# Attention backward on one core: halves of X's transposes in iterations 2 and 6, part G behind the transposes in three iterations, Z one step later, loads at other steps

## The chip, the core and the metric

The kernel runs on one core of a Trainium2 chip. The core has a matrix engine (PE, whose weight loads are shown as PEld), a vector engine (DVE), a scalar engine (ACT), a general engine (POOL) and a sequencer that issues DMAs (SP). Each engine works through its own instructions in the order in which the program lists them; between engines, order comes from semaphores only. The metric is the device time of one execution in microseconds, as a median of several runs.

## The reference

A gated attention block and its gradient, in bf16. `x` is 2048 x 512, there are 32 heads of 16 columns, and a feed-forward branch of 1792 gates the attention. The kernel returns the output and the gradients with respect to seven inputs.

```
def _A_ref(x, wqkv, wo):
    qkv = (x @ wqkv) split into 3, heads of 16
    scores = einsum("bhqd,bhkd->bhqk", q, k) * (Dh ** -0.5)
    p = softmax(scores)
    o = einsum("bhqk,bhkd->bhqd", p, v)
    return o @ wo
def _fwd_reference(...):
    xn = layernorm(x)
    s = _A_ref(xn, A_wqkv, A_wo)
    g = silu(layernorm-MLP of xn)
    return x + s * g
_out, _vjp = jax.vjp(_f, A_x, A_wqkv, A_wo, B_w1, B_b1, B_w2, B_b2)
_grads = _vjp(grad_out)
```

What matters here is the middle of the kernel: for each head, the 2048 x 2048 matrix of exponentials E, the matrix G = E * (dO V^T), and the sums over both that give the attention's output and the gradients of q, k and v.

## The kernel before

Three stages follow one another: a stage that makes q, k, v and the gate (up to 219 us), the attention (`attention_core`, from 219 to about 1867 us), and the weight gradients (`Grads.run`). The change is in the attention alone.

The attention works on pairs of heads (16 pairs) and, for each pair, on four groups of 512 queries: 64 **blocks**. A block has 16 **iterations**, one for each 128 keys (`kb`). The loop at L1382 runs over `g`, the number of the iteration over all blocks; "iteration k" below means `g % 16 == k`. The loop writes the order of all engines' work out by hand. In iteration g it emits, in this order:

- `emit_cO(g - 2)` (L1226): two DVE copies (L1233) of 128x64 words, for some g only ("older", below).
- `emit_xt(g - 1)` and `emit_fin(g - 1)`: for two g of a block, a DVE copy of a transposed half of X (L1292) and POOL's work on it (L1313 to L1331), which makes the weights W1 and W2 of Z.
- `emit_d` and `emit_s`: four PE products d, s, s, d with 32-row weights (L1137, L1115). s is of the next unit, g + 1; d is dO V^T of unit g. s has one PSUM tile; d has three in turn.
- `emit_exp(g + 1)`: ACT's exponential (L1124) into `ets`, which holds E of the last twelve units.
- `emit_z(g + ZOFF)` (L1352): four PE products Z with 32-column weights W on the transposed G (`gk`) and E (`ek`, `ekd`) of a unit 20 iterations back. Eight steps sum into one PSUM tile.
- `emit_x(g - 1, part)`: twelve PE products into X, in three parts: "e" (E with k and v, L1250, here called E part), "l" (row sums, L1253, L part) and "g" (the product tile `gts` of unit g - 1, L1257, G part). In iteration 1 all three come after the transposes instead of before them.
- `emit_T(g - 1)` (L1208): seven of the eight 128x128 transposes of unit g - 1's E, into the PSUM tile `tT`, of which there is one. `emit_XT(g)` (L1284) puts two fp32 transposes of a half of X into the second half of the same tile.
- `emit_mult(g)`: two DVE products (L1153), `gts` = d * E. Between the two, in some iterations, DVE copies X out (`emit_xs`, L1266, iteration 0) or adds Z to its accumulator (`emit_acc`, L1364 and L1366, when eight Z steps are done).
- Loads that are due: POOL reads a corner of `gts` (`tick`, L1422), so that it waits for unit g, and issues one DMA for the operands of the next pair of heads.
- `emit_cT(g - 1)` (L1224): ACT's copy of the transposes from `tT` to `ek`; and `emit_dmat(g)`: DMA transposes that SP issues, of G (`gk`, L1170, every second iteration) and of the tiles of E that PE leaves out (`ekd`, L1180 to L1186, at units 4, 6, 12 and 14).

Since `tT` has one buffer, the transposes of an iteration can start only when everything that reads the tile of the iteration before is done: ACT's copy, DVE's older copies and the copy of the half of X.

Two functions make room for the halves of X. `cut(g)` says for which units the first three transposes are left out, so that half of `tT` is free; `OLDER` says in which later units those three tiles are made up, one each, as an eighth transpose (L1211), and DVE copies that one and its neighbour (`emit_cO`). Units 16 and up do this, so the first block has neither.

```
OLDER = {2: (0, 0), 4: (0, 1), 5: (0, 2), 6: (3, 0), 7: (3, 1), 8: (3, 2)}
def cut(g):
    return 3 if g >= 16 and g % 16 in (0, 3) else 0
FIN_AT = {1: 1, 4: 0}
ZOFF = -20
```

The keys of `OLDER` are units; a unit u is transposed in iteration u + 1 and its older tile is copied by DVE in iteration u + 2. So eight transposes stand in iterations 3, 5, 6, 7, 8 and 9, four and a half of X in 1 and 4, and DVE's older copies in 4 and 6 to 10. `ZOFF` sets when Z of a block begins (iteration 4 of the next block) and so when a sum of eight is complete: in iterations 3 and 11.

The loads for the next pair are spread over its four blocks, four to a block, due at iterations 6, 9, 12 and 15 (L1395): 13 for most pairs, 128 KB each for the two `NATQ` tiles, 64 KB for most others, 264 KB for `NAT`. In the first block of a pair POOL also stores the finished gradients (L1370, L1373) behind the two accumulations.

Of the kernel before, what the change touches and what calls it, by code (L numbers as in the profile page):

```python
# [69 lines left out]
def natq_loads(k, t, p, ld):  # L70
    return [lambda n=n, d=d: ld(out=t[n][:].rearrange("q k j c -> q k (j c)"), in_=d[p])
            for n, d in (("NATQq", k.NATQq_s), ("NATQd", k.NATQd_s))]
# [978 lines left out]
def attention_core(ctx, ctx_r, tc, k, grads, Oall, dQall, dKVT_out, ident_f32, ident_bf, npairs=16, nqc=4):  # L1051
    nc = tc.nc
# [36 lines left out]
    st_s, st_d, st_et, st_gt, st_T = {}, {}, {}, {}, {}  # L1089
# [3 lines left out]
    def a_unit(g):  # L1093
        return (g // 16, g % 16) if 0 <= g < NSTEP else None
# [6 lines left out]
    def op_of(j):  # L1101
        return OP[blocks[j][0] % 2]
# [16 lines left out]
    def emit_exp(g):  # L1119

        a = a_unit(g)
        if a is None:
            return
        nc.scalar.activation(out=st_et[g][:, :, :, a[1] % 4, :].rearrange("k b h q -> k h b q"),  # L1124
                             in_=cur["s"][:].rearrange("k h (b q) -> k h b q", b=4), func=ACT.Exp)

    def emit_d(g, hj):
        a = a_unit(g)
        if a is None:
            return  # L1130
        j, kb = a
        op = op_of(j)
        qc = blocks[j][1]
        r = 64 + 32 * hj
        d = ps_d.tile([128, 512], f32, name="d", tag="d")
        st_d[g, hj] = d
        nc.tensor.matmul(d[:], lhsT=op["KVT"][r:r + 32, kb * 128:(kb + 1) * 128], rhs=op["QDT"][r:r + 32, qc * 512:(qc + 1) * 512],  # L1137
                         start=True, stop=True, tile_position=(r, 0))


    def emit_mult(g):
        a = a_unit(g)
        if a is None:
            emit_xs(g - 1)
            emit_acc(g + ZOFF)
            return
# [5 lines left out]
        for hj in range(2):  # L1152
# [3 lines left out]
            if hj == 0:  # L1156
                emit_xs(g - 1)
                emit_acc(g + ZOFF)

# [27 lines left out]
                                            in_=ets[:].rearrange("k s b h a q -> k (s b h) (a q)")[:, 8 * sl - 1:8 * sl + 1]  # L1187
                                            .rearrange("k x q -> k (x q)"))

    OLDER = {2: (0, 0), 4: (0, 1), 5: (0, 2), 6: (3, 0), 7: (3, 1), 8: (3, 2)}  # L1190

    def cut(g):
        return 3 if g >= 16 and g % 16 in (0, 3) else 0

    def older(g):
        return OLDER.get(g % 16) if 16 <= g < NSTEP else None

    def emit_T(g):
        a = a_unit(g)
        if a is None:  # L1200
            return
        kk = a[1] % 4
        et = st_et[g]
        t = ps_t.tile([128, 512], f32, name="tT")
        tb = t[:].bitcast(bf16).rearrange("q (i k) -> q i k", k=128)
        for i in range(cut(g), 7):
            b = i + a[1] // 4 % 2
            nc.tensor.transpose(tb[:, i - cut(g), :], et[:, b // 2, b % 2, kk, :], ident_bf[:])  # L1208
        if older(g):
            kk2, b = older(g)  # L1210
            nc.tensor.transpose(tb[:, 7, :], st_et[g // 16 * 16 + kk2][:, b // 2, b % 2, kk2, :], ident_bf[:])  # L1211
        st_T[g] = t
        if kk == 0:
            cur["ek"] = ekc.tile([128, 4, 7, 128], bf16, name="ek")
            blk[a[0]]["Ek"][a[1] // 4] = cur["ek"]
# [11 lines left out]
    def emit_cO(g):  # L1227
        if a_unit(g) is None or not older(g):
            return
        j, kb = a_unit(g)  # L1230
        kk, i = older(g)
        for (kc, x, y), c in (((kb // 4, kb % 4, 6), 384), ((0, kk, i), 448)):
            nc.vector.tensor_copy(out=blk[j]["Ek"][kc][:, x, y].bitcast(f32), in_=st_T[g][:, c:c + 64])  # L1233

    def emit_x(g, part):
        a = a_unit(g)
        if a is None:
            return
        j, kb = a
        if part == "e" and kb == 0:  # L1240
            blk[j]["X"] = ps_x.tile([128, 512], f32, name="X", tag="X")
        X = blk[j]["X"]
        NATt = op_of(j)["NAT"]
        et = st_et[g]
        for c in range(4):
            half, hj = c // 2, c % 2
            r = 32 * c
            ev = et[:, half::2, hj, kb % 4, :]
            if part == "e":
                nc.tensor.matmul(X[r:r + 32, 0:256], lhsT=NATt[:, kb, hj, 1:33], rhs=ev,  # L1250
                                 start=(kb == 0), stop=False, skip_group_check=True, tile_position=(0, r))
            elif part == "l":
                nc.tensor.matmul(X[r:r + 32, 256:512], lhsT=Lc[:], rhs=ev,  # L1253
                                 start=False, stop=False, skip_group_check=True, tile_position=(0, r))
            else:
                gv = st_gt[g][:, kb % 2, hj, :].rearrange("k (b q) -> k b q", b=4)[:, half::2, :]
                nc.tensor.matmul(X[r:r + 17, 256:512], lhsT=NATt[:, kb, hj, 0:17], rhs=gv,  # L1257
                                 start=False, stop=(kb == 15), skip_group_check=True, tile_position=(0, r))

    def emit_xs(g):  # L1260
        a = a_unit(g)
        if a is None or a[1] != 15:
            return
        j = a[0]
        xs = xsp.tile([128, 512], f32, name="xs", tag="xs")
        nc.vector.tensor_copy(out=xs[:], in_=blk[j].pop("X")[:])  # L1266
        blk[j]["xs"] = xs

    def fin_half(g):
        j = g // 16 - 1  # L1270
        at = FIN_AT if j < NB - 1 else FIN_END
        return (j, at[g % 16]) if 0 <= j < NB and g % 16 in at else None
# [14 lines left out]
    def emit_xt(g):  # L1287
        f = fin_half(g)
        if f is None:
            return  # L1290
        j, h = f
        nc.vector.tensor_copy(out=blk[j]["xs"][:, 256 * h:256 * h + 256], in_=blk[j].pop("XT"))  # L1292
# [62 lines left out]
    def emit_acc(g):  # L1355
        u = z_unit(g)
        if u is None or u[2] != 3 or u[3] != 1:
            return
        j, kp = u[0], u[1]
        p, qc = blocks[j]  # L1360
        Z = blk[j]["Z"]
        av = acc[:, kp, :]
        if qc == 0:
            nc.vector.tensor_copy(out=av, in_=Z[:])  # L1364
        else:
            nc.vector.tensor_tensor(out=av, in0=Z[:], in1=av, op=ALU.add)  # L1366
        if qc == nqc - 1:
            ob = (outp.tile([128, 512], bf16, name="ob") if kp == 0 or j < NB - 1 else
                  xsp.tile([128, 512], bf16, name="ob", tag="xs"))
            nc.gpsimd.tensor_copy(out=ob[:], in_=av)  # L1370
            dv = dKVT_out[p * 64:(p + 1) * 64, :].rearrange("r (a b s) -> r a b s", a=2, b=2)
            for b in range(2):
                nc.gpsimd.dma_start(out=dv[:, kp, b, :], in_=ob[b * 64:(b + 1) * 64, :])  # L1373

    FIN_AT = {1: 1, 4: 0}
    FIN_END = {1: 1, 2: 0}
    ZOFF = -20
    late = []
    for hj in range(2):
        emit_s(0, hj)  # L1380
    emit_exp(0)
    for g in range(NSTEP - ZOFF):  # L1382
        cur["g"] = g
        a = a_unit(g)
        if a is not None:
            j, kb = a
            p, qc = blocks[j]
            if kb == 0 and qc == 0:
                L = natq_loads(k, k.op0, p, nc.gpsimd.dma_start) if p > 0 else []
                if p + 1 < npairs:  # L1390
                    L += op_load_list(k, OP[(p + 1) % 2], p + 1, nc.gpsimd.dma_start)
                else:
                    L += grads.tail_loads(nc.gpsimd.dma_start)
                for i, f in enumerate(L):
                    late.append((g + 16 * (i // 4) + 6 + 3 * (i % 4), f))  # L1395
        emit_cO(g - 2)
        if a_unit(g - 2) is not None:
            emit_xt(g - 1)
            emit_fin(g - 1)
        emit_d(g, 0)  # L1400
        emit_s(g + 1, 0)
        emit_s(g + 1, 1)
        emit_d(g, 1)
        emit_exp(g + 1)
        emit_z(g + ZOFF)
        if g % 16 != 1:
            for part in "elg":
                emit_x(g - 1, part)
        st_T.pop(g - 2, None)
        emit_T(g - 1)  # L1410
        emit_XT(g)
        if g % 16 == 1:
            for part in "elg":
                emit_x(g - 1, part)
        emit_mult(g)
        if a_unit(g - 1) is None:
            emit_xt(g)
            emit_fin(g)
        for it in [x for x in late if x[0] <= g]:
            late.remove(it)  # L1420

            nc.gpsimd.tensor_copy(out=tick[:], in_=st_gt[g][0:1, kb % 2, 1, 510:512])  # L1422
            it[1]()
        if g >= NSTEP:
            grads.tail_mid(g - NSTEP)
        emit_cT(g - 1)
        emit_dmat(g)
        st_gt.pop(g - 2, None)
        st_et.pop(g - 12, None)
        if g == NSTEP:  # L1430
            ctx_r.close()
            grads.tail_open(ps_t, ps_s, ps_d)
# [113 lines left out]
```

## Time and profile before

| what | value |
|---|---|
| median of 3 runs | 2196.99 us (2195.66 to 2199.49) |
| profiled execution | 2192.31 us, span 2190.3 us |
| granted PE clock over the span | 0.998 |
| attention, first d of block 0 to first d of block 63 | 218.6 to about 1829.2 us |
| mean block, blocks 2 to 61 | 25.55 us, of it DVE 24.2, ACT 23.1, POOL 6.4 busy |
| DMA moved | 461.14 MB, most of it by SP's transposes |

The block and iteration times are read from the starts of the d products (L1137) in the trace: an iteration runs from its first d to the next iteration's first d. A busy PE is not a PE at its peak, since matmuls overlap and their ends are modelled; so starts are compared, not lengths. Idle time of an engine that nobody waits for costs nothing.

### The profile page before, as it was taken

The numbers are of one execution on the slowest core, as the hardware profiler recorded it, in microseconds if no ns is written. First come the engines' busy times: TensorE is split into PE (matmuls) and PEld (weight loads), VectorE is DVE, ScalarE is ACT, GpSimd is POOL, SyncE is SP. The second block draws the span as 40 slices with busy tenths as digits, with TensorE's granted clock in tenths as the row PEclk, the third lists the DMA queues.
The fourth block names the chain that finished last, engine by engine and source line by source line (L and its number), as shares of the span: only waits on it lengthen the run. The fifth ranks groups of instructions, "written<-read, shape, count | busy, mean of one in ns | idle before, by whom it ended". The sixth has DMA issues, their size and how long they took to land.

```text
span 2190.3 us, 74125 instructions
## 1 busy us (share of the span) xinstructions
PE 2138.8 (98%) x30610; PEld 1159.2 (53%) x30659; DVE 1937.1 (88%) x3901; ACT 1769.5 (81%) x2481; POOL 597.0 (27%) x1373
## 2 busy tenths in 40 slices
PE   6999999999999999999999999999999999899999
PEld 3444555555555555555555555555555555444444
DVE  6677899999999999999999999999999999798647
ACT  5664889998989999989999899999899998685224
POOL 4376213221222222222223222222222222611003
PEclk9999999999999999999999999999999999999999
DMA  7786999999999999999999999999999999999975
GB/s 234 247 279 202 199 201 196 200 200 200 196 202 201 201 203 202 201 191 209 193 202 206 194 202 205 196 206 202 200 197 206 192 215 201 311 260 231 248 214 179
DMA packets 1422035, 461.14 MB, mean 211 GB/s; under 512 B 1334591, under 2 KB 1405887, under 8 KB 1421697
## 3 DMA queue, kind: packets, MB, share of 16 engines
q1 hardware_dynamic: 1407392, 425.46, 103.0%
q0 software_dynamic: 12720, 29.37, 4.8%
q8 instruction: 240, 3.93, 0.8%
q10 hardware_dynamic: 1584, 1.57, 0.2%
q14 instruction: 99, 0.80, 0.1%
HBM read 62.79 MB, written 64.75 MB: 58 GB/s over the span
## 4 chain that ended last, share of the span: by engine, by line
PE 90%; DMA 4%; DVE 2%; ACT 2%; issue 1%; SPq 0%; POOL 0%; ACTq 0%; DVEq 0%; POOLq 0%
PE tT L1208 22%; PE Z L1352 15%; PE d L1137 15%; PE X L1257 5%; PE X L1250 5%; PE X L1253 5%; PE s L1115 3%; PE ps_dy L909 2%; DMA ekd<-ets 2%; PE ps_dw L983 2%; PE ps_h L352 2%; PE ps_m L367 2%; PE ps_dw L742 2%; PE ps_dh L875 2%; PE tT L1284 1%; PE ps_dxa L1027 1%
## 5 line engine op out<-in xcount | busy, mean ns | idle before, releaser
L1153 DVE TENSOR_TENSOR gts<-d,ets 128x512 bf16<-128x512 f32 x2048 | 1305.2, 681 | 73.0 <-issue 23.4
L1124 ACT ACTIVATE ets<-s 128x1024 bf16<-128x1024 f32 x1024 | 1049.3, 1025 | 44.7 <-ACT ek L1224 26.7
L1224 ACT COPY ek<-tT 128x448 f32<-128x448 f32 (+2 forms) x1024 | 504.8, 493 | 113.7 <-PE tT L1208 14.7
L1208 PE MATMUL tT<-ident_bf,ets 128*128 128x128 bf16 x6790 | 557.6, 221 | 0.0
L1208 PEld LDWEIGHTS <-ets 128*128 128x128 bf16 x6790 | 382.7, 98 | 223.3 <-issue 129.7
L1137 PE MATMUL d<-QDT,KVT 32*128 32x512 bf16 x2048 | 462.5, 383 | 0.0
L1115 PE MATMUL s<-QDT,KVT 32*128 32x512 bf16 x2048 | 401.4, 381 | 9.0 <-ACT ets L1124 9.0
L1257 PE MATMUL X<-gts,NAT 128*17 128x256 bf16 x4096 | 299.9, 273 | 0.0
L1250 PE MATMUL X<-ets,NAT 128*32 128x256 bf16 x4096 | 290.8, 274 | 0.0
L1253 PE MATMUL X<-ets,Lc 128*32 128x256 bf16 x4096 | 289.9, 273 | 0.0
L1352 PEld LDWEIGHTS <-W 128*32 128x32 bf16 x4096 | 105.4, 93 | 235.8 <-issue 233.6
L1352 PE MATMUL Z<-gk,W 128*32 128x512 bf16 x2048 | 203.6, 389 | 1.2 <-DVE acc L1366 1.0
L1352 PE MATMUL Z<-ek,W 128*32 128x512 bf16 x1792 | 203.6, 389 | 0.0
L1137 PEld LDWEIGHTS <-KVT 32*128 32x128 bf16 x2048 | 140.2, 91 | 117.7 <-issue 24.9
L1422 POOL COPY tick<-gts 1x2 bf16<-1x2 bf16 x205 | 36.2, 176 | 539.3 <-DVE gts L1153 535.0
L1253 PEld LDWEIGHTS <-Lc 128*32 128x32 bf16 x4096 | 109.8, 97 | 102.5
L1115 PEld LDWEIGHTS <-KVT 32*128 32x128 bf16 x2048 | 134.0, 91 | 22.8 <-issue 17.1
L1233 DVE COPY ek<-tT 128x64 f32<-128x64 f32 x756 | 133.9, 219 | 12.0 <-ACT ek L1224 1.4
L1313 POOL TENSOR_TENSOR W<-NATQq,rL 128x128 bf16<-128x128 bf16 x64 | 25.4, 398 | 428.9 <-DVE rL L1312 364.9
L1257 PEld LDWEIGHTS <-NAT 128*17 128x17 bf16 x4096 | 112.9, 91 | 13.7 <-issue 0.3
L1250 PEld LDWEIGHTS <-NAT 128*32 128x32 bf16 x4096 | 108.1, 96 | 15.0 <-issue 15.0
L1352 PE MATMUL Z<-ekd,W 128*32 128x512 bf16 x256 | 99.7, 389 | 0.0
(252 smaller groups left out, 2462.6 us busy)
## 6 DMA issues: line engine op xcount, KB each, us to landing
gk<-gts SPq DMA_TRANSPOSE x512, 5.4
H1T_s<-h1r SPq DMA_DIRECT2D x28, 256.0 KB, 4.3
HGT_s<-hgT SPq DMA_DIRECT2D x8, 896.0 KB, 4.4
DH_s<-stg SPq DMA_DIRECT2D x12, 512.0 KB, 3.7
hch<-DH_s SPq DMA_DIRECT2D x12, 512.0 KB, 5.3
gp<-H1T_s SPq DMA_DIRECT2D x9, 512.0 KB, 7.7
out_dram<-ob_w POOLq DMA_DIRECT2D x36, 128.0 KB, 4.4
NAT_s<-NS SPq DMA_DIRECT2D x4, 1056.0 KB, 6.2
```

What stands on the lines that cost most here:

```text
L352: nc.tensor.matmul(ps[:], lhsT=w1_sb[:, ic, fc * 128:(fc + 1) * 128], rhs=yT[:, ic, g * 512:(g + 1) * 512], start=(ic == 0), stop=(ic == I ...
L1115: nc.tensor.matmul(s[:, hj, :], lhsT=op["KVT"][r:r + 32, kb * 128:(kb + 1) * 128], rhs=op["QDT"][r:r + 32, qc * 512:(qc + 1) * 512], start ...
L1124: nc.scalar.activation(out=st_et[g][:, :, :, a[1] % 4, :].rearrange("k b h q -> k h b q"), in_=cur["s"][:].rearrange("k h (b q) -> k h b q ...
L1137: nc.tensor.matmul(d[:], lhsT=op["KVT"][r:r + 32, kb * 128:(kb + 1) * 128], rhs=op["QDT"][r:r + 32, qc * 512:(qc + 1) * 512], start=True, ...
L1153: nc.vector.tensor_tensor(out=gts[:, kb % 2, hj, :].rearrange("k (b q) -> k b q", b=4), in0=st_d.pop((g, hj))[:].rearrange("k (b q) -> k b ...
L1208: nc.tensor.transpose(tb[:, i - cut(g), :], et[:, b // 2, b % 2, kk, :], ident_bf[:])
L1224: nc.scalar.copy(out=blk[j]["Ek"][kb // 4][:, kb % 4, c:hi].rearrange("q i k -> q (i k)").bitcast(f32), in_=st_T[g][:, 0:(hi - c) * 64])
L1233: nc.vector.tensor_copy(out=blk[j]["Ek"][kc][:, x, y].bitcast(f32), in_=st_T[g][:, c:c + 64])
L1250: nc.tensor.matmul(X[r:r + 32, 0:256], lhsT=NATt[:, kb, hj, 1:33], rhs=ev, start=(kb == 0), stop=False, skip_group_check=True, tile_positi ...
L1253: nc.tensor.matmul(X[r:r + 32, 256:512], lhsT=Lc[:], rhs=ev, start=False, stop=False, skip_group_check=True, tile_position=(0, r))
L1257: nc.tensor.matmul(X[r:r + 17, 256:512], lhsT=NATt[:, kb, hj, 0:17], rhs=gv, start=False, stop=(kb == 15), skip_group_check=True, tile_pos ...
L1352: nc.tensor.matmul(Z[r:r + 32, :], lhsT=WT[j % 2][1 - part][:, qb, hj, :], rhs=mv, start=(part == 0 and qb == 0), stop=(part == 1 and qb = ...
```

## The change

Five things change, all in `attention_core`:

- The transposed halves of X go from iterations 1 and 4 to iterations 2 and 6 (`FIN_AT`), so the units that leave out three transposes are 1 and 5 instead of 0 and 3 (`cut`).
- Their three tiles each are made up in units 3, 6, 7 (of unit 1) and 8, 9, 11 (of unit 5) instead of 2, 4, 5 and 6, 7, 8. The indices in `emit_T` and `emit_cO` are generalized, because unit 5 is not in the first group of four.
- X: parts E and L always come before the transposes. Part G comes before them too, except in iterations 1, 5 and 13, where it comes after. Before, iteration 1 had all three after.
- `ZOFF` is -21, so each Z step comes one iteration later, the accumulations come in iterations 4 and 12, and the loop has one more step at its end.
- The loads of a block are due at iterations 4, 5, 11 and 12.

```
-    OLDER = {2: (0, 0), 4: (0, 1), 5: (0, 2), 6: (3, 0), 7: (3, 1), 8: (3, 2)}
+    OLDER = {3: (1, 0), 6: (1, 1), 7: (1, 2), 8: (5, 0), 9: (5, 1), 11: (5, 2)}

     def cut(g):
-        return 3 if g >= 16 and g % 16 in (0, 3) else 0
+        return 3 if g >= 16 and g % 16 in (1, 5) else 0
...
         if older(g):
-            kk2, b = older(g)
-            nc.tensor.transpose(tb[:, 7, :], st_et[g // 16 * 16 + kk2][:, b // 2, b % 2, kk2, :], ident_bf[:])
+            kk2, i = older(g)
+            b = i + kk2 // 4 % 2
+            nc.tensor.transpose(tb[:, 7, :], st_et[g // 16 * 16 + kk2][:, b // 2, b % 2, kk2 % 4, :], ident_bf[:])
...
-        for (kc, x, y), c in (((kb // 4, kb % 4, 6), 384), ((0, kk, i), 448)):
+        for (kc, x, y), c in (((kb // 4, kb % 4, 6), 384), ((kk // 4, kk % 4, i), 448)):
...
-    FIN_AT = {1: 1, 4: 0}
+    FIN_AT = {2: 1, 6: 0}
     FIN_END = {1: 1, 2: 0}
-    ZOFF = -20
+    ZOFF = -21
...
-                    late.append((g + 16 * (i // 4) + 6 + 3 * (i % 4), f))
+                    late.append((g + 16 * (i // 4) + (4, 5, 11, 12)[i % 4], f))
...
         emit_z(g + ZOFF)
-        if g % 16 != 1:
-            for part in "elg":
-                emit_x(g - 1, part)
+        emit_x(g - 1, "e")
+        emit_x(g - 1, "l")
+        if g % 16 not in (1, 5, 13):
+            emit_x(g - 1, "g")
         st_T.pop(g - 2, None)
         emit_T(g - 1)
         emit_XT(g)
-        if g % 16 == 1:
-            for part in "elg":
-                emit_x(g - 1, part)
+        if g % 16 in (1, 5, 13):
+            emit_x(g - 1, "g")
```

## The prediction

> **What bounds the kernel now.** I read the page first, then the waits, then one block of 16 iterations engine by engine, and last the DMA that ACT sometimes waits for. The first fence is from the page: engine totals, and the chain that ended last.
>
> ```profile
> span 2190.3 us, 74125 instructions
> PE 2138.8 (98%) x30610; PEld 1159.2 (53%) x30659; DVE 1937.1 (88%) x3901; ACT 1769.5 (81%) x2481; POOL 597.0 (27%) x1373
> ...
> PE 90%; DMA 4%; DVE 2%; ACT 2%; issue 1%; SPq 0%; POOL 0%; ACTq 0%; DVEq 0%; POOLq 0%
> ```
>
> PE carries the chain, so what counts is the order of PE's work and what holds it. One such hold is in the waits (who waited for whom: us in total, times, longest):
>
> ```profile
> PEld L1208 <- DVE ek L1233: 87.1, 378, 0.3
> ```
>
> 378 is 6 x 63: after each of the six "older" transposes of a block, the next group of transposes waits until DVE has copied the extra tile out of the one tT buffer. Next, PE in iterations 1, 4 and 13 of block 25 (start, length, instruction):
>
> ```profile
> 862.68 0.39 PE L1115 MATMUL s<-QDT,KVT 32*128 32x512 bf16 x2
> ...
> 863.00 0.40 PE L1352 MATMUL Z<-ek,W 128*32 128x512 bf16 x4
> 863.34 0.40 PE L1208 MATMUL tT<-ident_bf,ets 128*128 128x128 bf16 x4
> 863.57 0.39 PE L1284 MATMUL tT<-ident_f,xs 128*128 128x128 f32 x2
> 863.89 0.29 PE L1250 MATMUL X<-ets,NAT 128*32 128x256 bf16 x4
> ...
> 864.12 0.28 PE L1257 MATMUL X<-gts,NAT 128*17 128x256 bf16 x4
> 864.33 0.38 PE L1137 MATMUL d<-QDT,KVT 32*128 32x512 bf16 x1
> ...
> 868.24 0.35 PE L1257 MATMUL X<-gts,NAT 128*17 128x256 bf16 x4
> 868.57 0.40 PE L1208 MATMUL tT<-ident_bf,ets 128*128 128x128 bf16 x4
> ...
> 882.06 0.40 PE L1352 MATMUL Z<-gk,W 128*32 128x512 bf16 x4
> 882.28 0.28 PE L1250 MATMUL X<-ets,NAT 128*32 128x256 bf16 x4
> ...
> 882.50 0.28 PE L1257 MATMUL X<-gts,NAT 128*17 128x256 bf16 x4
> 882.72 0.56 PE L1208 MATMUL tT<-ident_bf,ets 128*128 128x128 bf16 x7
> 883.21 0.38 PE L1137 MATMUL d<-QDT,KVT 32*128 32x512 bf16 x1
> ```
>
> And DVE around iteration 4 of the same block:
>
> ```profile
> 866.98 0.68 DVE L1366 TENSOR_TENSOR acc<-Z,acc 128x512 f32<-128x512 f32 x1
> 867.57 0.68 DVE L1153 TENSOR_TENSOR gts<-d,ets 128x512 bf16<-128x512 f32 x1
> 868.17 0.34 DVE L1233 COPY ek<-tT 128x64 f32<-128x64 f32 x2
> ```
>
> The reader should see three things. First, the pitches. Z to X takes 0.22 us, but Z to T (862-864) takes 0.34; G to T takes 0.22 although G's own pitch is 0.11; G to the next d takes 0.21. Each change between the narrow X/Z shapes, the full 128x128 transposes and d costs about 0.10. An ordinary iteration has three such changes, iteration 1, with X behind T, has four. Second, iteration 13 is the floor, 1.48 us (881.73 to 883.21); iterations 0 and 15 take 1.55, because s waits for the exp of one step before (s starts 0.07 late). Third, in iteration 4 the queue on DVE is acc, product, copies; T starts at 868.57, just after the copies end at 868.51, 0.33 behind G instead of 0.22.
>
> Block 25 takes 25.32 us, and by position (0 to 15): 1.55, 1.72, 1.48, 1.64, 1.67, 1.555, 1.58, 1.58, 1.58, 1.58, 1.525, 1.555, 1.645, 1.48, 1.61, 1.55. The medians over blocks 2 to 61 are the same within 0.01. The mean block is 25.55; the difference is single long iterations, treated last.
>
> **The change, part by part**, for a steady block. Letters: T the seven transposes (0.50 to the next d), G the last part of X.
>
> *The halves of the transposed X* go from iterations 1 and 4 to 2 and 6. Four T and two fp32 transposes take 0.55 (868.57 to 869.12) against 0.50 for seven T: minus 0.055 in 1 and 4, plus 0.055 in 2 and 6. DVE copies one half in iteration 3 and one in 7 (0.34 each, and 0.2 for rL), where its queue is short; W1 and W2 are still two iterations ahead of the Z that uses them, as now.
>
> *The older tiles* are taken in iterations 4, 7, 8, 9, 10, 12 (now 3, 5, 6, 7, 8, 9), each 0.055 on PE; their copies run on DVE at 5, 8, 9, 10, 11, 13.
>
> *Z one step later* puts acc into DVE's queue in iterations 4 and 12 instead of 3 and 11, and the next Z waits for acc until 0.16 to 0.23 into the following iteration, before its own turn at 0.34. It adds one Z step to the tail: sixteen Z take about 0.9 there, 0.22 for four.
>
> *G behind T* in 1, 5 and 13 gives each a fourth change of shape. In 1 this replaces all of X behind T.
>
> Now the two places that decide. **Iteration 5**: DVE runs iteration 4 as product 0.49, acc 1.09, product 1.69; in iteration 5's time (4 lasts 1.61) the copies of the older tile can start at 0.68 and end at 1.03, T starts at 1.09 (0.06 later, as at 868.57). PE was ready for it at Z 0.34 + E, L 0.34 + 0.22 = 0.89. In the old order G (from 0.82, when its product lands) would fill this hole and the iteration would end at 1.09 + 0.50 = 1.59. In the new one G comes after: 1.09 + 0.50 + 0.21 = 1.80. **Iteration 13** is the same with the older tile of iteration 12 behind the acc of 12: products and acc at 0.56, 1.16, 1.76, copies from 0.74 to 1.09, T 1.15, end 1.86. Before, no older tile lay behind the second acc.
>
> *Iteration 1*: s 0.07, Z 0.395, E 0.62, L 0.73, T 0.945, G 1.44, end 1.65; G's product ends at 0.92, so the new order has no wait.
>
> The block after, by position: 1.55, 1.654, 1.539, 1.529, 1.607, 1.796, 1.539, 1.585, 1.58, 1.58, 1.58, 1.52, 1.61, 1.859, 1.484, 1.584. In 2, 6 and 14 s does not wait for exp, so they are at the PE floor, 1.48, plus 0.055 where X is transposed; in 3 and 7 it waits 0.05; 8 to 10 stay at 1.58, the round from T by ACT's and DVE's copies back to T. Against the medians now: 1: -0.068; 2: +0.058; 3: -0.116; 4: -0.068; 5: +0.241; 6: -0.043; 7: +0.002; 10: +0.055; 11: -0.035; 12: -0.036; 13: +0.376; 14: -0.127; 15: +0.031; the rest nothing. Together +0.27. Times 63 blocks +17.0, block 0 (no older tiles, two more shape changes) +0.2, tail +0.2: **+17.4 us**.
>
> Bounds of the unknown: T to G has no row; the nearest are the fp32 transposes to E in iteration 1 (863.57 to 863.89, the same 0.32 as to d in iteration 4) and G to d (0.21). I take these; below, the added change of shape could be free (0), above it is 0.12. At 0 the sum loses 3 x 0.10 x 63 = 19. The Trainium skill, TensorE: Matmul & The Clock Gate, Part 2 (step 4, DRAIN), gives about 128 cycles for the last wavefront to leave the array, an estimate of 0.053 us at the 2.4 GHz of that page, by which each added change would cost half and the sum would be +8. The trace differs: 0.10 at each of the four changes of iteration 1.
>
> *Loads*: POOL's tick and load pairs (0.18 + 0.5 to 0.6) move from 6, 9, 12, 15 to 4, 5, 11, 12, beside POOL's 27% busy. What they touch is the ekd transpose on SP. It reads E, and exp of four to five iterations later overwrites E:
>
> ```profile
> DMA to landing us min/median/max: 3.0/4.5/7.4
>   ACT ets L1124: 4.4, 7
> ```
>
> (the ekd line's own view). It is issued in iteration 7 or 8 and must have landed by 11.5, about 5.8 us; a second one is issued in 15 or 0, for exp in iteration 3. The 25 iterations that are over 0.12 us longer than their median, in blocks 1 to 62, hold 11.3 us, most in 12 and 4. In blocks 4, 16, 28 and 52 a 128 KB load was issued 0.2 after ekd and ekd took 6.5 to 7.4; in blocks 12, 24 and 36, where the load went 0.1 to 0.3 ahead, 3.5 to 4.0. After the change no load is issued in iterations 7 to 11 except where POOL is late behind the output stores (0.57 each) of every fourth block, and none near the second ekd. Bounds: all stalls go (-11.3), or the two loads in a row hold the gk transposes ahead of ekd and as much is added (+11). I take -4, nearer to the blocks with the load ahead of ekd.
>
> **Sum.** +17.4 - 4 = +13.4. The profiled execution took 2192.31, of it 2190.3 span, so 2205.7 for such an execution; it lies 4.7 under the median of the three timed runs, 2196.99, and against that the forecast is **2210**.
>
> **Rivals.**
> (1) *The loads were the point*: all 11.3 us of stalls go, +6.1: 2203. For it: the four blocks above; against it: stalls also in blocks 10, 34 and 39, with other loads. 0.10.
> (2) *Faster*: the fourth change of shape costs nothing, as T's last columns drain beside G. Place: iterations 1, 5, 13. 2210 - 19 = 2191. It decides once a change costs under 0.01 (faster by 0.2% needs 2192.6, 17.4 of 19 gone). Against it: 0.21 from G to d in iteration 1. 0.05.
> (3) *Half*: a change behind T costs 0.05, because one of T's two edges hides in the next weights' load: 2210 - 9.5 = 2200.5. Against it: the same row, and 0.32 behind the fp32 transposes whether E or d follows. 0.05. This is also where the drain of the Trainium skill's page TensorE: Matmul & The Clock Gate, Part 2, would put it.
> (4) *T isn't held by the copies in 5 and 13*, which would save 0.20 + 0.27 a block: 2210 - 29 = 2181. Against it: 378 of 378 older tiles were waited for. 0.04.
> (5) *Worse queueing*: the loads at 4 and 5 delay SP's transposes, and stalls double: 2210 + 15 = 2225. 0.08.
>
> **How the numbers follow.** My case has 0.68, over 2201 to 2216 (-8 to +3 on stalls, 0.04 a block either way on the sums). About 0.2% (4.4 us) is what a measurement of this kernel can tell from no change. Faster: rivals 2 and 4 and an edge of the third, 0.10. Same (2192.6 to 2201.4): rival 3, some of rival 1 and the low end of mine, 0.12. Slower: 0.78. The range leaves out 2 in 10, about half at each end: 2199 to 2218.
>
> **What would show it.** Right: block mode near 25.6; iteration 13 the longest at about 1.86 and 5 at 1.80, with T waiting for the DVE copies of ek in both; G to d 0.21 in 1, 5 and 13; iteration 14 at 1.48; ACT waiting for ekd less than now. Wrong: T in iteration 5 starting at 0.9, G following T without the 0.10, or long iterations at 12 that grow.

## The result, and the profile after

Five executions of the changed kernel have a median of 2226.52 us (2225.08 to 2235.92), five of the kernel before 2196.99 (2194.77 to 2199.49). The ratio is 1.014, 95% interval 1.0123 to 1.0157: slower by 1.4%, clear of the noise. The forecast was 2210 and its range ended at 2218; the side was right, the size was less than half of what came (+13 against +29.5), and the measured time lies outside the range. The profiled execution of the changed kernel is the slowest of its five, 2235.92 with a span of 2234.0, so 9.4 of its difference to the profile before is not in the median.

The page of the changed kernel, engine totals:

```profile
span 2234.0 us, 74090 instructions
PE 2149.4 (96%) x30610; PEld 1146.8 (51%) x30659; DVE 1953.5 (87%) x3901; ACT 1787.7 (80%) x2481; POOL 597.4 (27%) x1373
```

PE has the same number of instructions as before and 10.6 us more busy time; the span has 43.7 more. The rest is PE standing still. The waits (who waited for whom: us in total, times, longest):

```profile
PEld L1208 <- DVE ek L1234: 123.1, 377, 0.5
...
DVE xs L1293 <- ACT ek L1225: 30.7, 125, 0.4
```

The first line was 87.1 before. The second has no counterpart there. It is seen in the rows of the copy of the half of X (line, engine, operation, tiles, count | busy us, mean ns of one | idle before it, and what ended it), first before, then after:

```profile
L1292 DVE COPY xs<-tT 128x256 f32<-128x256 f32 x126 | 52.9, 420 | 0.7
```

```profile
L1293 DVE COPY xs<-tT 128x256 f32<-128x256 f32 x126 | 53.5, 425 | 30.8 <-ACT ek L1225 30.7
```

Where the two halves stood before, DVE came to the copy late and found it ready; 0.7 us of idle time in 126 copies. In iterations 3 and 7 DVE comes early and waits, 0.17 and 0.28 us (medians), for ACT to finish its own copy out of the same `tT` tile.

The iterations by position (medians over blocks 2 to 61, us, from the starts of the d products in the trace; the positions that are left out lie within 0.01 of the forecast):

| iteration | before | forecast | after |
|---|---|---|---|
| 1 | 1.722 | 1.654 | 1.659 |
| 2 | 1.481 | 1.539 | 1.540 |
| 3 | 1.645 | 1.529 | 1.529 |
| 4 | 1.675 | 1.607 | **1.772** |
| 5 | 1.554 | 1.796 | **1.859** |
| 6 | 1.582 | 1.539 | 1.539 |
| 12 | 1.646 | 1.61 | 1.611 |
| 13 | 1.483 | 1.859 | **1.899** |
| 14 | 1.611 | 1.484 | 1.482 |
| block of 16 | 25.33 | 25.60 | 25.89 |

Thirteen of the sixteen positions are where the forecast put them. PE in iterations 1, 4 (one line, its second d) and 5 of block 25 of the changed kernel (start, length, instruction):

```profile
873.90 0.56 PE L1208 MATMUL tT<-ident_bf,ets 128*128 128x128 bf16 x7
874.39 0.29 PE L1258 MATMUL X<-gts,NAT 128*17 128x256 bf16 x4
874.62 0.39 PE L1137 MATMUL d<-QDT,KVT 32*128 32x512 bf16 x1
...
877.94 0.37 PE L1137 MATMUL d<-QDT,KVT 32*128 32x512 bf16 x1
...
880.12 0.28 PE L1254 MATMUL X<-ets,Lc 128*32 128x256 bf16 x4
880.60 0.56 PE L1208 MATMUL tT<-ident_bf,ets 128*128 128x128 bf16 x7 [0.20 <-DVE ek L1234]
881.09 0.29 PE L1258 MATMUL X<-gts,NAT 128*17 128x256 bf16 x4
881.31 0.38 PE L1137 MATMUL d<-QDT,KVT 32*128 32x512 bf16 x1
```

From G to the next d it is 0.23 and 0.22: the fourth change of shape costs what was forecast. In iteration 5, T stands 0.48 behind the L part and PE waits for DVE's older copies. This is DVE over iterations 3 (from 876.15), 4 (from 877.68) and 5 (from 879.46) of the same block:

```profile
876.66 0.42 DVE L1293 COPY xs<-tT 128x256 f32<-128x256 f32 x1 [0.17 <-ACT ek L1225]
877.12 0.20 DVE L1313 RECIPROCAL rL<-xs 128x8 f32<-128x8 f32 x1
877.24 1.84 DVE L1153 TENSOR_TENSOR gts<-d,ets 128x512 bf16<-128x512 f32 x3
879.00 0.68 DVE L1367 TENSOR_TENSOR acc<-Z,acc 128x512 f32<-128x512 f32 x1
879.60 0.69 DVE L1153 TENSOR_TENSOR gts<-d,ets 128x512 bf16<-128x512 f32 x1
880.19 0.35 DVE L1234 COPY ek<-tT 128x64 f32<-128x64 f32 x2
```

From 876.66 to 880.54 DVE has no gap. It starts the copy of the half 0.17 late, rL (the reciprocal that W is made from), which reads the copy, starts only after the copy's end, and the first product of iteration 3 begins 1.09 into the iteration. It ends in iteration 4, and the second d of iteration 4, which takes over its d tile, starts only then (877.94, 0.26 into the iteration; iteration 4: 1.77). The older copies, for which T of iteration 5 waits, end at 880.54 (iteration 5: 1.86). The copy of the other half in 7 waits as well and costs nothing: 7 and 8 are at 1.587 and 1.581, as forecast.

The view of ekd, what waited for it and how long it took:

```profile
  ACT ets L1124: 9.9, 7
...
DMA to landing us min/median/max: 2.6/4.3/5.9
```

The exponential's waits for ekd grew from 4.4 to 9.9 us, though the longest transfer became shorter (7.4 to 5.9). The single long iterations (over 0.12 above their median, blocks 1 to 62) hold 14.8 us, against 11.3 before.

### The profile page after: what moved, and what is told of

The parts are those of the page before. It is cut to its first block, busy times and chain, and to the rows that moved or that the text cites. A ratio compares the mean times of both kernels' runs of the same rounds, so it can differ in the third digit from the quotient of the medians.

```text
span 2234.0 us, 74090 instructions
## 1 busy us (share of the span) xinstructions
PE 2149.4 (96%) x30610; PEld 1146.8 (51%) x30659; DVE 1953.5 (87%) x3901; ACT 1787.7 (80%) x2481; POOL 597.4 (27%) x1373
## 5 line engine op out<-in xcount | busy, mean ns | idle before, releaser
L1258 PE MATMUL X<-gts,NAT 128*17 128x256 bf16 x4096 | 291.1, 274 | 0.0
L1137 PEld LDWEIGHTS <-KVT 32*128 32x128 bf16 x2048 | 134.0, 91 | 117.7 <-issue 21.8
L1115 PEld LDWEIGHTS <-KVT 32*128 32x128 bf16 x2048 | 127.4, 91 | 20.9 <-issue 17.1
L1258 PEld LDWEIGHTS <-NAT 128*17 128x17 bf16 x4096 | 103.2, 91 | 21.8 <-issue 0.2
```

Source lines behind the costliest of these rows:

```text
L1115: nc.tensor.matmul(s[:, hj, :], lhsT=op["KVT"][r:r + 32, kb * 128:(kb + 1) * 128], rhs=op["QDT"][r:r + 32, qc * 512:(qc + 1) * 512], start ...
```

## The experiments

Block times are sums of the sixteen medians, and long iterations are sums over blocks 1 to 62, both from the one profiled execution of each kernel; "before" ran beside them on the same chips at 2198 to 2200, where nothing else is said.

**G behind T in iteration 1 alone.** Of the changed kernel:

```
-        if g % 16 not in (1, 5, 13):
+        if g % 16 not in (1,):
...
-        if g % 16 in (1, 5, 13):
+        if g % 16 in (1,):
```

> The changed kernel, with part G behind the transposes in iteration 1 alone; in 5 and 13 it stands ahead of them again. Theory: in 5 and 13 the transposes wait for DVE's older copies anyway, so G ahead of them fills the hole, and G behind them adds its whole 0.21. Then iteration 5 goes from 1.86 to about 1.65 and 13 from 1.90 to about 1.69; 6 and 14 give back some 0.07 each because s waits for exp again. Block of medians from 25.89 to about 25.54, the time from 2226.5 to about 2204. Rival: only the added change of shape counts, 0.10 in each of the two: block 25.7, time 2214.

Measured: 2211.58 (2204.0 to 2212.72), ratio to before 1.0051 (1.0036 to 1.0066), block 25.504, iteration 5 at 1.641, iteration 13 at 1.681. So G behind T in 5 and 13 costs 0.39 a block, 15 us between the medians, half of the loss. Long iterations hold 18.4 us here, more than in either kernel; they took back some of the gain.

**The first half of X in iteration 1**, with the places of the tiles left out to fit:

```
-    OLDER = {3: (1, 0), 6: (1, 1), 7: (1, 2), 8: (5, 0), 9: (5, 1), 11: (5, 2)}
+    OLDER = {3: (0, 0), 6: (0, 1), 7: (0, 2), 8: (5, 0), 9: (5, 1), 11: (5, 2)}
...
-        return 3 if g >= 16 and g % 16 in (1, 5) else 0
+        return 3 if g >= 16 and g % 16 in (0, 5) else 0
...
-    FIN_AT = {2: 1, 6: 0}
+    FIN_AT = {1: 1, 6: 0}
```

> The changed kernel with the first half of X transposed in iteration 1 instead of 2 (so its three missing tiles are those of unit 0, made up in the same units 3, 6, 7); all else as changed, G behind the transposes in 1, 5 and 13 too. Theory: in iteration 3 of the changed kernel DVE waits for ACT's copy out of the same tT tile before it can copy the half of X, which pushes the products and holds the second d of iteration 4 (a d tile is free only after its product). With the half in iteration 1, ACT's copy is over before DVE gets there, so iteration 4 falls from 1.77 to about 1.57, 1 and 3 rise by 0.05 to 0.09, block 25.89 to about 25.70, time about 2214. Rival: iteration 4 is long for another reason (Z one step later, acc in 4, POOL's work on the half), then it stays at 1.77 and the block at 25.9.

Measured: 2228.54 (2225.94 to 2232.43), ratio 1.0135 (1.0113 to 1.0158), block 25.976. Iteration 4 fell to 1.54, but 3 rose to 1.74 and 5 to 1.97. The copy starts at 0.38 of iteration 2 here, rL at 0.89 and the product at 1.02: the same queue, one iteration earlier, holds d in 3 instead of 4. So the hold of d moves with the copy; it doesn't go. And it doesn't need the wait: DVE waits for ACT's copy 0.00 in the median here, as the theory had it, and the copy and rL alone push the product this far. Iteration 5 is long for another reason. DVE has a gap ahead of the first product of 4 (0.31 in block 25), which starts at 0.59; the older copies behind the acc of 4 come no sooner for it, and since 4 is shorter, T of 5 waits for them longer.

**Halves in 1 and 5, older copies away from acc, G behind T in 1 alone.**

```
+    OLDER = {1: (0, 0), 5: (0, 1), 6: (0, 2), 7: (4, 0), 8: (4, 1), 13: (4, 2)}
...
+        return 3 if g >= 16 and g % 16 in (0, 4) else 0
...
+    FIN_AT = {1: 1, 5: 0}
...
```

> A version that should beat both, if the two holds are the whole story: halves of X in iterations 1 and 5, older tiles made up in units 1, 5, 6 and 7, 8, 13, so that DVE's older copies come in iterations 3, 7 to 10 and 15 and none right behind an accumulation (4 and 12); G behind the transposes in iteration 1 alone; Z one step later and the loads as changed. Theory: iterations 4 and 13 fall to about 1.52 and 1.59, block about 25.16 against 25.33 before and 25.89 changed, time about 2180. Rival: the cost lies in Z one step later or in the loads, which this kernel keeps: then it is at 2197 or above.

A miss: 2223.91 (2221.33 to 2224.78), ratio 1.0111 (1.009 to 1.0132), block 25.506. There were holds in 3 (1.70), 5 (1.82) and 13 (1.70). The one in 3 is the known one: copy, rL and product at 0.39, 0.90 and 1.04 of iteration 2, and the second d of 3 not before 0.24. In 5 and 13 no older copy stands, but part G waits for its product there: the product behind the acc of 4 or 12 ends 0.99 and 0.93 into the iteration, and T, behind G, starts at 1.26 and 1.20 (medians). So to keep the older copies away from acc doesn't free T while G stands ahead of it. And the long iterations hold 29.7 us, with ACT waiting 19.9 us for ekd: what a shorter block gains is in part lost again where the exponential comes to ekd sooner.

**The parts alone, on the kernel before.** The loads at 4, 5, 11, 12; Z one step later (`ZOFF = -21`); the halves in 2 and 6 with the changed `OLDER` and `cut`.

```
+                    late.append((g + 16 * (i // 4) + (4, 5, 11, 12)[i % 4], f))
```

> The kernel before with the loads alone moved to iterations 4, 5, 11 and 12. Theory: the medians by position stay, block 25.33; the single long iterations (11.3 us in blocks 1 to 62 of the profiled run before, most of them at 12) fall to about 4, time about 2190. Rival: the loads in a row hold SP's transposes, long iterations grow to 15 or more, as in the changed kernel's profiled run (14.8), time 2197 to 2205.

```
+    ZOFF = -21
```

> The kernel before with Z one step later alone, so that the accumulations come in iterations 4 and 12. Theory, by the holds found so far (DVE's queue, the one tT tile, the three d tiles): in iteration 4 the accumulation now follows the older copies, in 5 the copy of the half of X comes last in DVE's queue and the transposes wait for it; iteration 5 goes from 1.55 to about 2.1, 4 and 12 shrink by 0.1, block 25.33 to about 25.75, time about 2225. Rival, as the prediction had it: Z one step later costs only its step in the tail, time about 2200.

```
+    OLDER = {3: (1, 0), 6: (1, 1), 7: (1, 2), 8: (5, 0), 9: (5, 1), 11: (5, 2)}
...
+        return 3 if g >= 16 and g % 16 in (1, 5) else 0
...
+    FIN_AT = {2: 1, 6: 0}
```

> The kernel before with the halves of X in iterations 2 and 6 and the older tiles that go with them, and nothing else. Theory: the half's DVE copy in iteration 3, behind ACT's copy, meets the accumulation of iteration 3; the products come late and hold d, and iterations 4 and 12 are about 2.2 and 2.05; block about 26.15, time about 2250. So this part alone is worse than the whole change, and Z one step later gives half of it back. Rival: the parts add up, halves cost 0.1 to 0.2 a block, time about 2205.

Measured: loads 2203.05 (2198.07 to 2209.3), ratio 1.002 (1.0004 to 1.0036), block 25.346, long iterations 22.7 us: in this execution, which took 6.0 us more than the median of its ten, the loads at these steps add stalls and take none away; the medians, 3.0 us apart, point the same way. Z 2219.92 (2218.8 to 2228.17), ratio 1.0102 (1.0069 to 1.0135), block 25.716 with iteration 5 at 2.106. Halves 2239.84 (2238.75 to 2240.93), ratio 1.0181 (1.0141 to 1.0222), block 26.146 with iteration 4 at 2.219 and 12 at 2.062. The block times of the last two came as written. The time of the halves was 10 below, with only 2.6 us in long iterations: a longer block gives ekd more time to land.

The parts don't add. Loads, Z and halves alone lengthen the block by 0.02, 0.39 and 0.82; all three together, with G behind T in 1, by 0.17 (25.504 in the first experiment). With the halves moved alone, Z of iteration 4 waits for acc, which stands behind the copy of the half; with Z alone, acc stands behind the older copies. Moved together they pass each other.

**The half not read.** The first half of X is filled with ones by DVE and not copied out of the PSUM tile, so the kernel leaves out this half of X. The fill takes 0.27 where the copy took 0.42, and it reads nothing that ACT reads, so the wait and a part of the length go together:

```
+        XT = blk[j].pop("XT")
+        if h == 1 and j < NB - 1:
+            nc.vector.memset(blk[j]["xs"][:, 256 * h:256 * h + 256], 1.0)
+            return
...
```

> The changed kernel, in which DVE fills the first half of X with ones instead of copying it from the tT tile (so the weights W of Z, and the outputs that hang on them, are not the reference's); with no read of the tile, DVE need not wait for ACT's copy out of it. Theory: in iteration 3 the fill starts at about 0.2 instead of 0.51, the products come 0.35 earlier, the second d of iteration 4 is not held, iteration 4 falls from 1.77 to about 1.61 and 5 from 1.86 to about 1.80, 13 stays at 1.90, block 25.89 to about 25.66. Rival: iteration 4 is held by something else and stays at 1.77.

Measured once: 2222.01, block 25.76. Iteration 4 is at 1.607, the forecast's own number. Iteration 5, though, is 1.90, not 1.80; the cause is found below.

**The loads back at 6, 9, 12, 15**, all else as changed.

> The changed kernel with the loads back at iterations 6, 9, 12 and 15. Theory: medians by position as changed, except 13, where no product waits for POOL's tick eight units back any more (first product of 12 at 0.49 instead of 0.59): 1.90 to about 1.865; long iterations about as many as before, 10 us; time 2226.5 to about 2222. Rival: the loads at 4, 5, 11 and 12 were a gain, the time grows by 4 or more.

Measured: 2229.31 (2222.06 to 2231.88), ratio 1.0128 (1.0091 to 1.0166), block 25.837. Iteration 13 fell from 1.899 to 1.858, the forecast's 1.859; the time, however, didn't fall. The medians of the first product's start show what happened: with the loads at 4, 5, 11 and 12 it starts at 0.59 in iterations 2 and 12, with the loads back it starts at 0.48 and 0.56 there and at 0.59 in 0 and 6. The `tick` ahead of a load reads the `gts` buffer that the products of eight iterations later write again, so the first product that writes it waits for POOL too.

**rL behind the first product of iteration 3.** On the changed kernel, `emit_fin` of the first half is issued inside `emit_mult`:

```
             if hj == 0:
+                if a_unit(g - 2) is not None and (fin_half(g - 1) or (0, 0))[1] == 1:
+                    emit_fin(g - 1)
                 emit_xs(g - 1)
...
```

> The changed kernel, with rL and the W products of iteration 3 issued behind the first product of d instead of ahead of it. In the changed kernel the copy of the half waits for ACT (0.51), rL follows at 0.97, the product at 1.09, and the second d of iteration 4 is held until 0.26. Theory A (this hold is the cost): the product starts at 0.85, iteration 4 falls from 1.77 to 1.61, iteration 5 stays 1.86, block 25.73, about 2216. Theory B (VectorE runs without a gap from the copy in iteration 3 to the older copies in iteration 5, and T of iteration 5 waits for the last of them, so the order within this queue buys nothing): iteration 4 falls to 1.61 and iteration 5 rises by the same 0.16 to 2.02, block 25.89, about 2226. I hold B.

Measured: 2226.04 (2218.95 to 2230.37), ratio 1.0113 (1.0091 to 1.0135), block 25.765: iteration 4 at 1.609, iteration 5 at 1.904. DVE in iterations 3 to 5 (the first from 873.72):

```profile
874.23 0.42 DVE L1295 COPY xs<-tT 128x256 f32<-128x256 f32 x1 [0.17 <-ACT ek L1227]
874.57 0.68 DVE L1153 TENSOR_TENSOR gts<-d,ets 128x512 bf16<-128x512 f32 x1
875.16 0.19 DVE L1315 RECIPROCAL rL<-xs 128x8 f32<-128x8 f32 x1
...
877.64 0.35 DVE L1236 COPY ek<-tT 128x64 f32<-128x64 f32 x2
```

Neither theory was quite right. Iteration 5 did rise, as B says, since T there waits for the end of the queue; but by 0.045 and not 0.16, for the queue itself became 0.12 shorter (copies 3.92 behind the start of iteration 3, not 4.04). A product that doesn't read the copy starts 0.34 behind its start, before it ends; rL, which reads it, starts 0.46 behind. It is the reading, not the kind of instruction: the same rL behind a product that it doesn't read starts 0.09 before that product ends (875.16 against 874.57 + 0.68). The order of the queue has a price after all: 0.12 for an instruction that needs the one just ahead of it. Between the medians nothing is seen of the 8 us that 0.125 a block would be; the part after the attention was 6 us longer in the profiled execution than in that of the changed kernel, and the executions spread over 11 us.

**Both causes away: the half not read, and the loads back; then the load of 12 at 11.**

```
+                    late.append((g + 16 * (i // 4) + 6 + 3 * (i % 4), f))
```

> The changed kernel with two things away at once: the first half of X is filled with ones and not read from the PSUM tile (its outputs are not the reference's), and the loads stand at 6, 9, 12 and 15 as before. If the copy of the half and the loads' ticks are all that the forecast of the block had wrong, every position returns to it: iteration 4 at 1.61, 5 at 1.80 (the first product of 4 at 0.49, not 0.59), 13 at 1.86, block 25.60; about 2213. Rival (something else holds T in 5): 5 stays at 1.90 and the block at 25.72.

```
+                    late.append((g + 16 * (i // 4) + (6, 9, 11, 15)[i % 4], f))
```

> The half filled with ones and not read, as before, and the loads at 6, 9, 11 and 15. A load's tick on POOL reads the buffer that the product of 8 iterations later writes (the even one of the pair), so these four make the first product of 14, 0, 2 and 6 wait for POOL too; a load at 12, which both kernels have, makes that of 4 wait, and there it starts at 0.59, not 0.49. Theory (that wait, though long since met, costs 0.10 and T of 5 gets it): the first product of 4 starts at 0.49, iteration 5 falls from 1.90 to 1.80, 13 stays at 1.86, block 25.62, about 2207. Rival (something else holds T in 5): 5 stays at 1.90 and the block at 25.73.

Measured, once each: 2214.69 (the kernel before beside it once, 2191.69), block 25.727, iteration 5 at 1.902, 13 at 1.860; and 2217.43, block 25.618, iteration 5 at 1.792, 13 at 1.859. In the first, the rival was right; in the second, the theory. DVE of the first (iteration 4 from 872.60), and then of the second (iteration 4 from 871.92):

```profile
871.72 1.25 DVE L1153 TENSOR_TENSOR gts<-d,ets 128x512 bf16<-128x512 f32 x2
873.19 0.69 DVE L1153 TENSOR_TENSOR gts<-d,ets 128x512 bf16<-128x512 f32 x1 [0.22 <-POOL W L1323]
873.79 0.68 DVE L1371 TENSOR_TENSOR acc<-Z,acc 128x512 f32<-128x512 f32 x1
874.39 0.68 DVE L1153 TENSOR_TENSOR gts<-d,ets 128x512 bf16<-128x512 f32 x1
874.99 0.35 DVE L1234 COPY ek<-tT 128x64 f32<-128x64 f32 x2
```

```profile
871.16 1.93 DVE L1153 TENSOR_TENSOR gts<-d,ets 128x512 bf16<-128x512 f32 x3
873.01 0.68 DVE L1371 TENSOR_TENSOR acc<-Z,acc 128x512 f32<-128x512 f32 x1
873.61 0.68 DVE L1153 TENSOR_TENSOR gts<-d,ets 128x512 bf16<-128x512 f32 x1
874.21 0.35 DVE L1234 COPY ek<-tT 128x64 f32<-128x64 f32 x2
```

With a load at 12 the first product of iteration 4 starts at 0.59, behind a wait that the profile puts down to POOL; with the load at 11 it runs on from the two of iteration 3, at 0.48. The copies that T of 5 waits for start 0.79 and 0.68 into iteration 5. The tick in question had run eight iterations earlier, so the wait was long met; and the product doesn't need the W that the profile names. The first kernel shows by itself that it is this wait: the fourth block of a pair has only one load, so every fourth block follows one without a load at 12. In these 15 of the 60 blocks one semaphore instruction stands on DVE between the product before and this one, this product starts at 0.48 and iteration 5 takes 1.78; in the other 45 there are two, and it is 0.59 and 1.90. The earlier run with the half not read has the same 1.78 and 1.90 in iteration 5. In the second kernel every position is within 0.01 of the forecast's list. So the half's copy in 3 (with its wait) and the ticks account for the whole miss of the block. The single times of these two kernels tell less: the second has 15.9 us in long iterations and the first 8.6.

**The kernel before with the first ekd tile in a DMA of its own.** In two groups of three, exp waits for a DMA that carries two tiles and is issued two iterations after the first of them is complete.

```
-            if sl == 0:
-                nc.sync.dma_start_transpose(out=ek[:, 0], in_=ets[:, 2, 3, 1].rearrange("k a q -> k (a q)"))
+            nc.sync.dma_start_transpose(out=ek[:, 0], in_=ets[:, (sl - 1) % 3, 3, 1].rearrange("k a q -> k (a q)"))
...
+            nc.sync.dma_start_transpose(out=ek[:, 1], in_=ets[:, sl, 0, 0].rearrange("k a q -> k (a q)"))
```

> The kernel before, with the first of the two tiles of ekd transposed by a DMA of its own, two iterations earlier, in every group (now: in one of three; the other groups send both in one DMA, and exp waits for it). If the long iterations are exp waiting for the combined ekd: block unchanged at 25.33, the long iterations' 11.3 us fall to 2 or 3, 2188. Rival (SP's queue is full, and two more issues of 1.2 us in every three blocks push the transposes of gk and the other ekd back by as much): the long iterations stay or grow, 2197 to 2205.

Measured: 2225.86 (2224.59 to 2227.77), ratio 1.012 (1.0099 to 1.0141), block 25.518, long iterations 38.9 us, 33.6 of them in 1, 2, 3 and 15. In its waits:

```profile
DVE gts L1153 <- DMA gk<-gts: 57.8, 62, 2.7
```

The rival was right, and too mild. exp doesn't wait for ekd at all any more (4.4 us before), but the transposes of G are pushed back on SP, their `gts` buffers are not free, and DVE's product waits for them: 1.2 us in two waits before, 58 now. The row of these transposes in the kernel before (ns per issue on SP: least, median, most):

```profile
L1170 SPq DMA_TRANSPOSE gk<-gts x512: 1584/2228/5203, 228.6 to 1857.9; - x171
```

Eight a block at 2.23 us and 171 in 64 blocks of ekd at some 1.25 make about 21 us of a block's 25.5, an estimate from medians; all the times of SP's transposes in the trace add up to 22.8 us of a mean block's 25.55. The split makes the 171 to 256, and the sum to 24.8 of 26.06. (The expectation counted two more in three blocks; it is four.) From issue to landing the transposes of G take 5.4 us in the median in both kernels, so it is the issue that comes late: SP's queue is the thing that is nearly full. The Trainium skill, DMA: Bandwidth & Descriptors, Issuing engines are not separate DMA queues, calls an engine's time to initiate a DMA usually small relative to the DMA itself. Here it is 2.2 us against 5.4 to landing, and with 85 more issues it bounds the schedule.

**Older tiles out of the iteration of acc, on the kernel before**; and the same with the split.

```
-    OLDER = {2: (0, 0), 4: (0, 1), 5: (0, 2), 6: (3, 0), 7: (3, 1), 8: (3, 2)}
+    OLDER = {4: (0, 0), 5: (0, 1), 6: (0, 2), 7: (3, 0), 8: (3, 1), 12: (3, 2)}
```

> The kernel before, with the older tiles transposed in iterations 5, 6, 7, 8, 9 and 13 instead of 3, 5, 6, 7, 8, 9: none has its copies behind acc. If T is held in iteration 4 by the copies (1.12 instead of 1.00): iteration 3 falls from 1.64 to 1.59, 4 from 1.67 to 1.55, 13 rises to 1.54, 14 falls to 1.56; block 25.16, 2187. Rival: in iteration 4 G is late itself (its product ends at 0.80, as G's end at 1.14 shows), so 4 stays near 1.65 and the block falls by 0.06 only: 2193, and more long iterations at 4 and 12 as the block grows shorter take that back: 2197. I hold the rival.

> Both edits, the older tiles in 5, 6, 7, 8, 9 and 13 and the first ekd tile in a DMA of its own. If the shorter block's gain is eaten by exp waiting for the combined ekd and the split frees it: block 25.27 (or 25.16, as above) and long iterations of 2 to 4 us, 2184. Rival (SP's queue is what is full): long iterations of 15 us or more and 2197 or above.

Measured: 2195.86 (2190.86 to 2200.7, 12 executions) against 2198.39 beside it, ratio 0.9982, interval 0.9969 to 0.9995, block 25.27 as the rival had it, with iteration 3 at 1.589 and 4 still at 1.685, long iterations 14.7 us. Iteration 4 stays long because G is late: its product ends at 0.86, and T follows G at 1.13 with no copies to wait for. This is the fastest kernel of the study, though only by about what a measurement can tell from no change. With the split: 2221.5 (2215.59 to 2238.05), ratio 1.0109 (1.008 to 1.0139), block 25.427, long iterations 38.4 us, as its rival had it.

## Why the prediction was right and wrong

**G behind T** (three times a fourth change of shape, 0.10 each): right. G to d is 0.22 to 0.23 in the trace, and the first experiment gives back 0.39 a block when 5 and 13 lose it, part change of shape, part the hole that G no longer fills. Rivals 2 and 3 fall with it, and so does the estimate of 0.053 worked out from the Trainium skill's page TensorE: Matmul & The Clock Gate, Part 2: the measured change of shape is about twice that.

**T held by the older copies in 5 and 13** (so rival 4 is out): right in kind, 377 waits of PE for DVE's copies, and in 13 right to 0.04. The sign that was read for it in the kernel before, T of iteration 4 just behind the copies, was weak: with the copies elsewhere that iteration stays at 1.685, because G is late too. What makes the hold costly in the new order is that G doesn't stand in the hole; with G ahead of T and no copies at all, iteration 13 is still 1.70 (the third experiment).

**The halves**: this is the step that failed. It said that "DVE copies one half in iteration 3 and one in 7 (0.34 each, and 0.2 for rL), where its queue is short", and took the products of iteration 4 from 0.49 on as if nothing stood ahead of them. The copy takes 0.42 (its row before said 420 ns; 0.34 is the distance to a next instruction that doesn't read it), it starts 0.17 later than DVE is free, since it waits for ACT's copy out of the same tile, and rL, which reads it, comes after its end. The queue doesn't drain until iteration 5: +0.165 in 4 and, on top of the forecast, +0.063 in 5. How much of it is the wait and how much the copy with rL, no run parts. An estimate from the rows: 0.17 sooner, the first product of 3 (0.65 long, from 1.09) would end 0.04 into iteration 4, and its second d would start about where it does when it isn't held (0.08), so in this place the wait decides; with the half in iteration 1 the copy and rL held d without it. The row before could not show the wait, for there DVE always came later than ACT (0.7 us idle in 126 copies); that the two read one tile stood in the code. The Trainium skill, PSUM — Partial Sum Buffer, PSUM bank collisions raise a hardware error, says that the compiler's scheduler adds a dependency between instructions on different engines that touch the same bank and quadrant, reads included. The trace agrees with such an order, 125 waits of 0.25 us in the mean; no run here has the two copies at once, so whether the chip could do it is not shown.

**The loads**: "I take -4" was wrong in sign, as far as one profiled execution of each kernel shows. Long iterations went up by 3.5 us with the change and by 11.4 with the loads alone; with the loads back on the changed kernel they are 12.0, but the median there didn't fall. What was missed beside that is the tick: a load at 12, 4 or 11 makes the first product of iteration 4, 12 or 2 wait for POOL, 0.03 to 0.11. In 13 that is the +0.04, and in 5 it is 0.11 that the late copy of the half hid. Why exp waits longer for ekd with loads at these steps wasn't settled: SP's queue is nearly full, and in the kernel before ekd took longer to land where a 128 KB load was issued just behind it (6.5 to 7.4 us against 3.5 to 4.0), but the runs don't part the two.

**Z one step later** was listed with a price of next to nothing beside acc's place in the queue. Alone it costs 0.39 a block and the halves alone 0.82; it is only the pair that comes near to even. The forecast had the pair right because it wrote DVE's queue out for the new order and didn't add parts.

**The sum.** The block is 0.29 over the forecast, 18.5 us in 63 blocks. The long iterations are +3.5 where -4 was said, 7.5. The part after the attention is 341.1 us, 5.35 longer, though of its code only Z's extra step changed, forecast at 0.2; it lay between 335.8 and 347.2 over all kernels here, and between 335.8 and 341.3 over those with Z where it was, so I don't count it as a term of the change. The start is 1.0 later and the first block 1.1 shorter than forecast. Together 31, against 30.2 by which the profiled execution (2235.92 to 2192.31, 43.6) exceeded +13.4. The medians differ by 29.5, because that execution lies 9.4 above its median and the one before 4.7 below. Which terms were smaller in the other four executions is not seen, as only one of them has a trace. Rival 5 gave 2225 and came near to the time for another reason: stalls did not double.

## What to carry to other kernels

Before a copy is moved to where "the queue is short", look for who else reads its source: a wait that never shows, because the engine always came late, appears when it comes early. Price the copy with the instruction that reads it, and not alone: without any wait the two held PE as well. Follow an in-order engine's queue until it has a gap again; a late start is paid wherever the next engine waits for that queue, not where it arose: here in 4 and 5 for a copy in 3, and nowhere for the one in 7. And a helper that only reads a corner of a buffer to pace something adds a wait to whoever writes that buffer next.

## What was not expected of the hardware

A DVE instruction that reads what the one just ahead of it writes starts 0.12 us later than one that doesn't (0.46 against 0.34 behind a copy of 0.42). A wait of DVE on POOL that had been met eight iterations earlier still moved the product's start by 0.11 us (0.59 against 0.48) where DVE had no backlog to hide it; the trace shows one more semaphore instruction on DVE ahead of the product in just these blocks. And SP's queue of DMA transposes, 2.2 us of issue for each large one, is so full that 85 more issues of 1.2 us in 64 blocks cost 27 us, by way of buffers that come free too late.
